# DeltaNet and a multiplicative FFN: the last unit's last two products in two PSUM tiles instead of the two halves of one

## The chip, the cores and the metric

The kernel runs on one core of a Trainium2 chip. The metric is device time in microseconds (us), measured around one execution of the program; the profile is one profiled execution of the same program. Engines are named as the profile names them: PE is the matmul engine (PEld its weight loads), DVE the vector engine, ACT the scalar engine, POOL GpSimd, SP the engine whose queue issues most DMAs.

## What is computed

An attention block (the delta rule, a recurrence over 768 tokens for 4 batches of 8 heads of 48 features) gives a matrix x of 3072 tokens by 384 features. A feed-forward block follows. The change is at the end of the second block:

```python
state = state + bt * einsum('bhd,bhe->bhde', kt, vt - v_old)   # for each token; y = q @ state before it
x = attn_out.transpose(0, 2, 1, 3).reshape(3072, 384)
a = x @ w1                    # 384 x 1024
b = x @ w2
h = a * b @ w3                # 1024 x 1024
out = h @ w_out               # 1024 x 384
```

All arrays are 32-bit floats.

## The kernel before, in words

The sequence is cut into 12 chunks of 64 tokens. Two chunks of all four batches make a unit `u` of 512 tokens, and there are six units (0 to 5; `last` is 5, L893). For a chunk the kernel computes scores, an inverse and the state; for a unit it then does the feed-forward part. The weights `w3` and `w_out` are multiplied together once, into `w34` (1024 x 384), so that a unit's output is (a * b) @ w34.

`ab` (L772) computes a * b of a unit in eight slabs of 128 features, each 128 x 512. PE makes both factors (L779), ACT copies the first one to SBUF (L791), and DVE multiplies it with the second (L795).

The product with `w34` is done by a scheme with seven products of halves in place of eight (a Strassen scheme). The tokens are cut into two halves `z`, the 1024 features into two halves `f`, and the 384 outputs into two halves `d` of 192. `slab_sums` (L835) makes sums of slabs in place on POOL (L846), `weight_sums` (L810) has made those of the weights once for all units. `o` (L851) lists the seven products, one per step: B11, T4, B21, T1, T2, T3, B22 by the name of the weight. Each is eight matmuls, two blocks of 128 tokens times four blocks of 128 features, accumulated over the features into one PSUM bank (L875). The profile lists two rows of 128x192 for each of these matmuls, so 16 rows make one product.

The products go into banks with one-letter names. In units 0 to 4 there are A (B11 and then B21 added), D (T4), C (T1 and then B22 added) and B (T2 and then T3 added). In the last unit T3 and B22 aren't added to B and C but have places of their own, E and F (L861, L862). E and F come from `two_banks` (L146), which gives a tile of two banks by turns out of two such tiles (the profile calls them ps_w); all the others come from `bank` (L149), one bank by turns out of four (ps_f). Before the change, one call of `two_banks` at E serves both, E as its first bank and F as its second.

`result` (L898) combines the banks on ACT and DVE. In the last unit its steps are, in this order:

- M1 = A after its first product, copied by ACT (L904), and osb(0,0) = A, complete, by ACT (L906), with its store
- U2 = M1 + B, U3 = U2 + E, M1 = U2 + C (all on DVE, L900)
- osb(1,1) = U3 + C, with its store
- osb(1,0) = U3 - D, with its store
- osb(0,1) = M1 + F, with its store

Each `store` (L882) writes a 128 x 384 tile osb, of which there are two, taken by turns, and sends it out with two DMAs on SP's queue (L888). So osb(0,1) takes the tile that osb(1,1) had.

The order of all the work is written out by hand in `ORDER` (L39): each name is a generator, and each mention runs it to its next `yield`. `in_text_order` (L159) then ties each engine's instructions to the order in which they were issued. At the end of the list the steps of the last unit are

```python
... o5 S5 S5 S5 o5 x5 S5 x5 o5 x5 x5 x5 x5 x5 x5 x5 x5
```

where `o5` is a product, `x5` a step of `result` and `S5` a slab sum. The three mentions of `o5` shown here make T2, T3 and B22: F's product stands ahead of U3 = U2 + E in the text. Waits between engines are set by the framework, from the tiles that an instruction reads and writes.

Of the kernel before, what the change touches and what calls it, by code (L numbers as in the profile page):

```python
# [89 lines left out]
def kernel(  # L90
# [47 lines left out]
    def in_turn(pool, shape, tag, n, name, dt=FP32):  # L138

        i = turns.get(tag, -1)  # L140
        while True:
            i = turns[tag] = (i + 1) % n
            if (tag, i) not in held:
                return pool.tile(shape, dt, tag=f"{tag}{i}", name=name, bufs=1)

    def two_banks():  # L146
        return in_turn(psW, [P, 2, 512], "w", 2, "ps_w")

    def bank(shape):  # L149
        return in_turn(psF, shape, "f", 4, "ps_f")  # L150
# [179 lines left out]
    def by_tensor(m, i, src):  # L330
        KQ = KQs[m] if m in KQs else new_KQ(m)
        ps = [bank([P, NR, NP, C]) for z in range(2)]
        for r in range(NR):
            for h in range(H):
                for z in range(2):
                    x = half(z if i else (z + h) % 2)
                    pe.matmul(
                        ps[z][feat(h % 2), r, h // 2, :], lhsT=src[x, r, h, :],
                        rhs=ident[x, x], start=True, stop=True,
                    )  # L340
        yield
        for z in range(2):
            for e in range(2):
                o = KQ[feat(e), NR * z : NR * z + NR, :, i, :].rearrange("p b a t -> p (b a) t")
                x = ps[z][feat(e)].rearrange("p r a t -> p (r a) t")
                if i or e:
                    act.copy(out=o, in_=x)  # L347
                else:
                    dve.tensor_copy(out=o, in_=x)
                yield  # L350
# [69 lines left out]
    def inverse(j):  # L420
# [15 lines left out]
        for s in range(BS - 1):  # L436
            n = BS - 1 - s
            t = in_turn(work, [P, 256], "tb", 2, "tb")
            tv = t[:, 0 : (s + 1) * n].rearrange("p (r t) -> p r t", t=n)
            dve.tensor_tensor(  # L440
                out=tv, in0=V[:, 0 : s + 1, s : s + 1].to_broadcast([P, s + 1, n]),
                in1=U[:, s, s + 1 : BS].unsqueeze(1).to_broadcast([P, s + 1, n]), op=ALU.mult,
            )
            o = V[:, 0 : s + 1, s + 1 : BS]
            dve.tensor_tensor(out=o, in0=o, in1=tv, op=ALU.subtract)  # L445
            yield
# [353 lines left out]
    HB, HF, HD = B // 2, KF // 2, DM // 2  # L800
# [48 lines left out]
    banks = {}  # L849

    def o(u):  # L851
        for z, f, w, n, first in (
            (0, 0, "B11", "A", True),
            (1, 1, "T4", "D", True),
            (0, 1, "B21", "A", False),
            (1, 0, "T1", "C", True),
            (0, 0, "T2", "B", True),
            (1, 1, "T3", "B", False),
            (0, 1, "B22", "C", False),
        ):  # L860
            if u == last and n + w in ("BT3", "CB22"):  # L861
                first, n = True, {"T3": "E", "B22": "F"}[w]  # L862
            if first and n in "EF":
                if n == "E":
                    extra = two_banks()
                banks[u, n] = extra[:, "EF".index(n), 0 : HB * HD].rearrange(
                    "p (b d) -> p b d", b=HB
                )
            elif first:
                banks[u, n] = bank([P, HB, HD])[:]  # L870
            ps = banks[u, n]
            for b in range(HB):
                t0 = (HB * z + b) * P
                for i in range(HF):
                    pe.matmul(  # L875
                        ps[:, b, :], lhsT=abs_[u, HF * f + i][:, t0 : t0 + P], rhs=ws_[w][:, i],
                        start=first and b == i == 0,
                        stop=i == HF - 1 and b == HB - 1, skip_group_check=not first,
                    )
            yield  # L880
# [156 lines left out]
```

## Time and profile before

| what | value |
|---|---|
| device time, three runs | 595.52, 597.24, 598.57 us (median 597.24) |
| the profiled execution | 599.28 us |
| its span, first to last instruction | 597.5 us |
| granted PE clock, mean | 0.976 |
| one product of `o` in the last unit, 16 rows | 2.76 us |
| one sum at L900, 128x384 | 0.55 us |
| end of PE's last matmul | 590.0 us from the span's start |
| last DMA issue on SP | begins at 594.72 us, takes 0.43 us |

The span is what the profile covers; the device time of the same execution has 1.78 us more around it. In the views below, a row gives an engine, a line of the kernel, what was written from what by the names of the tiles (with the number of a tile left out), the shape and a count. "Idle before" is how long the engine stood still ahead of a row, with the releaser that ended it. A chain of waits is followed back from the last instruction, at each step to what released it. Matmul ends are modelled.

### The profile page before, as it was taken

Reading aid. Unit: us, or ns where it says so; the run is one execution under the profiler, and the core shown is the slowest. Engines: PE = TensorE matmul, PEld = TensorE weight load, DVE = VectorE, ACT = ScalarE, POOL = GpSimd, SP = SyncE. Lnnn points to the kernel's source line nnn. Section 1 sums busy time; section 2 is a strip of 40 time slices with the busy share of each in tenths; the row PEclk is TensorE's granted clock in tenths of the full one; section 3 lists DMA queues with packets and bytes.
Section 4 is the critical chain, followed back from the end, with each engine's and each line's share of the span. In section 5 each row is a group of like instructions: output and inputs, shape, how many; then the busy total and the mean of one; then the engine's idle time right before and its main releaser. Section 6 shows DMA issues by size and latency. Waiting matters only on the chain.

```text
span 597.5 us, 19061 instructions
## 1 busy us (share of the span) xinstructions
PE 543.5 (91%) x8188; PEld 378.7 (63%) x8188; DVE 362.0 (61%) x827; ACT 158.8 (27%) x333; POOL 176.3 (30%) x223
## 2 busy tenths in 40 slices
PE   2468998768999999999999989999999999999994
PEld 2355555647888864559844669545697456964484
DVE  3797897659987478753895645865738915110112
ACT  3575353444512301121111212112220112301000
POOL 7553543114355502117011043111170002500060
PEclk9998999879999999999999989999999999999998
DMA  9988986767757454663544335624532030010001
GB/s 245 190 172 257 189 181 134 128 133 160 157 79 101 100 85 106 88 99 46 138 67 89 49 55 105 122 61 59 80 74 69 33 56 4 19 51 0 1 13 40
DMA packets 219507, 57.31 MB, mean 96 GB/s; under 512 B 206656, under 2 KB 212800, under 8 KB 219424
## 3 DMA queue, kind: packets, MB, share of 16 engines
q1 hardware_dynamic: 215232, 55.31, 46.4%
q10 hardware_dynamic: 4192, 0.79, 1.0%
q8 instruction: 64, 1.05, 0.8%
q14 instruction: 19, 0.16, 0.1%
HBM read 43.88 MB, written 11.01 MB: 92 GB/s over the span
## 4 chain that ended last, share of the span: by engine, by line
PE 74%; DMA 9%; DVE 6%; SPq 4%; ACT 3%; issue 3%; POOL 1%; DVEq 0%; ACTq 0%; POOLq 0%
PE ps_f L779 38%; PE ps_f L875 18%; PE ps_w L551 5%; PE ps_w L652 4%; PE ps_w L498 3%; PE ps_f L759 2%; DMA raw<-in_moe_w_dram 2%; DMA raw<-in_moe_w_out_dram 2%; DMA xT<-xT 2%; PE ps_w L367 2%; PE ps_w L373 1%; SPq L202 1%; DVE ps_w L445 1%; DVE tb L440 1%; DMA Vd<-Vb 1%
## 5 line engine op out<-in xcount | busy, mean ns | idle before, releaser
L779 PE MATMUL ps_f<-xT,w2s 128*128 128x512 f32 (+1 forms) x336 | 133.2, 543 | 0.8 <-POOL w2s L715 0.8
L779 PE MATMUL ps_f<-xT,w1s 128*128 128x512 f32 (+1 forms) x336 | 128.1, 533 | 1.6 <-DMA xT<-xT 1.6
L846 POOL TENSOR_TENSOR ab<-ab 128x256 f32<-128x256 f32 x96 | 67.2, 729 | 190.2 <-DVE ab L795 167.4
L779 PEld LDWEIGHTS ps_f<-xT,w1s 128*128 128x128 f32 x336 | 63.2, 190 | 56.7 <-issue 53.2
L779 PEld LDWEIGHTS ps_f<-xT,w2s 128*128 128x128 f32 x336 | 62.7, 191 | 55.4 <-issue 51.1
L791 ACT COPY ab<-ps_f 128x512 f32<-128x512 f32 (+1 forms) x56 | 28.2, 527 | 169.5 <-PE ps_f L779 163.3
L875 PE MATMUL ps_f<-w,ab 128*128 128x192 f32 x368 | 65.2, 331 | 0.1
L875 PEld LDWEIGHTS ps_f<-w,ab 128*128 128x128 f32 x368 | 59.7, 190 | 4.1 <-issue 3.2
L795 DVE TENSOR_TENSOR ab<-ab,ps_f 128x512 f32<-128x512 f32 (+1 forms) x56 | 32.7, 603 | 47.2 <-PE ps_f L779 47.1
L440 DVE TENSOR_TENSOR tb<-Vb,Ub 128x31 f32<-128x31 f32 (+15 forms) x124 | 45.4, 366 | 18.2 <-DMA Ub<-Ud 14.9
L759 PE MATMUL ps_f<-w2s,w3T 128*128 128x384 f32 x128 | 45.1, 504 | 4.5 <-POOL w2s L715 2.4
L875 PE MATMUL ps_f<-room,ab 128*128 128x192 f32 x272 | 48.0, 330 | 0.8 <-DVE room L900 0.8
L445 DVE TENSOR_TENSOR Vb<-Vb,tb 128x31 f32<-128x31 f32 (+15 forms) x124 | 45.0, 363 | 4.3
L875 PEld LDWEIGHTS ps_f<-room,ab 128*128 128x128 f32 x272 | 44.1, 190 | 1.6 <-issue 1.1
L673 ACT COPY xT<-ps_w 48x256 f32<-48x256 f32 x96 | 30.5, 366 | 52.9 <-PE ps_w L652 52.4
L759 PEld LDWEIGHTS ps_f<-w2s,w3T 128*128 128x128 f32 x128 | 24.3, 197 | 21.1 <-POOL w2s L715 3.4
L270 POOL TENSOR_TENSOR sq<-ktok 128x384 f32<-128x384 f32 x24 | 20.4, 852 | 56.0 <-DVE Vb L445 26.9
L367 PE MATMUL ps_w<-KQ 48*64 48x128 f32 x384 | 29.9, 292 | 1.1 <-ACT KQ L347 1.1
L715 POOL TENSOR_TENSOR w<-w,raw 128x512 uint32<-128x512 uint32 x16 | 20.8, 1305 | 34.1 <-DVE w L711 21.2
L373 PE MATMUL ps_w<-KQ 48*64 48x64 f32 x768 | 30.3, 232 | 0.1
L537 POOL TENSOR_TENSOR vtok<-vtok,n 128x384 f32<-128x384 f32 x24 | 20.2, 852 | 33.6 <-DMA vtok<-in_v_dram 33.6
L373 PEld LDWEIGHTS ps_w<-KQ 48*64 48x64 f32 x768 | 27.3, 145 | 0.4 <-ACT KQ L347 0.3
(110 smaller groups left out, 658.7 us busy)
## 6 DMA issues: line engine op xcount, KB each, us to landing
raw<-in_moe_w_dram SPq DMA_DIRECT2D x16, 512.0 KB, 6.6
vtok<-in_v_dram SPq DMA_DIRECT2D x24, 192.0 KB, 4.3
raw<-in_moe_w_dram SPq DMA_DIRECT2D x24, 192.0 KB, 4.4
out_dram<-osb SPq DMA_DIRECT2D x48, 96.0 KB, 2.4
ktok<-in_k_dram SPq DMA_DIRECT2D x44, 96.0 KB, 3.8
raw<-in_moe_w_out_dram SPq DMA_DIRECT2D x8, 384.0 KB, 3.8
Ud<-U SPq DMA_DIRECT2D x48, 64.0 KB, 2.7
Ub<-Ud SPq DMA_DIRECT2D x6, 512.0 KB, 4.0
```

Of the source, the lines that this page charges most:

```text
L367: pe.matmul(ps[half(z), 0, n : n + 128], lhsT=x[:, 0, :], rhs=x.rearrange("p j t -> p (j t)"), start=True, stop=True,)
L373: pe.matmul(ps[half(z ^ j), 1, n + C * j : n + C * j + C], lhsT=x[:, 0, :], rhs=x[:, j, :], start=True, stop=True,)
L440: dve.tensor_tensor(out=tv, in0=V[:, 0 : s + 1, s : s + 1].to_broadcast([P, s + 1, n]), in1=U[:, s, s + 1 : BS].unsqueeze(1).to_broadcast( ...
L445: dve.tensor_tensor(out=o, in0=o, in1=tv, op=ALU.subtract)
L551: pe.matmul(out(ps, r, h, z), lhsT=lhs(r, h, z), rhs=rhs(r, h, z), start=True, stop=True,)
L673: act.copy(out=xT[f, p:NP:2, b : b + NR, cc, :].rearrange("p a r t -> p r a t"), in_=pyv[f, z, b : b + NR],)
L759: pe.matmul(ps[:, 0:DM], lhsT=w3Ts[jc, kc // 4][:, kc % 4 * P : kc % 4 * P + P], rhs=wo[:, kc], start=(kc == 0), stop=(kc == KF - 1),)
L779: pe.matmul(ps[:].rearrange("p b c t -> p b (c t)"), lhsT=w[:, m, js], rhs=x[:, m, :, c0:c1].rearrange("p b c t -> p b (c t)"), start=(m = ...
L791: act.copy(out=t, in_=ps)
L795: dve.tensor_tensor(out=t, in0=t, in1=ps, op=ALU.mult)
L846: pool.tensor_tensor(out=o_, in0=x_, in1=y_, op=op)
L875: pe.matmul(ps[:, b, :], lhsT=abs_[u, HF * f + i][:, t0 : t0 + P], rhs=ws_[w][:, i], start=first and b == i == 0, stop=i == HF - 1 and b = ...
```

## The change

E and F each get a `two_banks` tile of their own, and each uses the first bank of it. Since these tiles come by turns out of two, E gets one of them and F the other. The list of steps is the same.

```diff
@@ -861,9 +861,7 @@
             if u == last and n + w in ("BT3", "CB22"):
                 first, n = True, {"T3": "E", "B22": "F"}[w]
             if first and n in "EF":
-                if n == "E":
-                    extra = two_banks()
-                banks[u, n] = extra[:, "EF".index(n), 0 : HB * HD].rearrange(
+                banks[u, n] = two_banks()[:, 0, 0 : HB * HD].rearrange(
                     "p (b d) -> p b d", b=HB
                 )
             elif first:
```

Lines behind the change move up by two.

## The prediction

> **What bounds the kernel now.** I read the page's busy shares first, then the chain of waits over the last 38 us, then the waits and the timeline of the last 23 us, then the busy time in single stretches of it.
>
> ```profile
> PE 543.5 (91%) x8188; PEld 378.7 (63%) x8188; DVE 362.0 (61%) x827; ACT 158.8 (27%) x333; POOL 176.3 (30%) x223
> PE 74%; DMA 9%; DVE 6%; SPq 4%; ACT 3%; issue 3%; POOL 1%; DVEq 0%; ACTq 0%; POOLq 0%
> ```
>
> PE sets the pace nearly everywhere: 91% busy and 74% of the chain. A change that leaves PE's work alone can only gain where PE isn't the end of the chain. The chain's last pieces show such a place:
>
> ```profile
> 584.79 5.21 PE ps_w L875 x32
> 590.00 0.02 issue
> 590.02 0.07 DVE room L900
> ...
> 590.96 0.56 DVE osb L900
> ...
> 591.91 1.73 DMA out_dram<-osb
> ...
> 593.76 0.55 DVE osb L900
> ```
>
> (Columns: start, length, what.) PE's last product ends at about 590.0 and the span at 597.5. In these 7.5 us PE has nothing to do: DVE makes the last sums, a store lands, DVE makes the very last sum, and it is stored too. This tail is what the change touches. The timeline shows when its parts start:
>
> ```profile
> 584.62 2.76 PE L875 MATMUL ps_w<-room,ab 128*128 128x192 f32 x16
> 584.88 0.56 DVE L900 TENSOR_TENSOR room<-room,ps_f 128x384 f32<-128x384 f32 x1 [12.37 <-PE ps_f L875]
> ...
> 587.22 2.76 PE L875 MATMUL ps_w<-w,ab 128*128 128x192 f32 x16
> 590.02 0.55 DVE L900 TENSOR_TENSOR room<-room,ps_w 128x384 f32<-128x384 f32 x1 [4.59 <-PE ps_w L875]
> 590.50 0.55 DVE L900 TENSOR_TENSOR room<-room,ps_f 128x384 f32<-128x384 f32 x1
> 590.96 1.01 DVE L900 TENSOR_TENSOR osb<-room,ps_f 128x384 f32<-128x384 f32 x2
> 593.76 0.55 DVE L900 TENSOR_TENSOR osb<-room,ps_w 128x384 f32<-128x384 f32 x1 [1.79 <-DMA out_dram<-osb]
> ```
>
> The first PE row is product E (weight T3), the second F (weight B22); both carry the name ps_w because they are halves of one tile. DVE's sum U3 = U2 + E stands in the fifth row. E is complete at 584.62 + 2.76 = 587.38 and U2 at 584.88 + 0.56 = 585.44, yet the sum starts at 590.02, just after F's end at 587.22 + 2.76 = 589.98. It reads nothing of F. So it waits 2.6 us for a product that it doesn't need; the waits put 4.6 us of DVE's idle time down to ps_w.
>
> ```profile
> DVE room L900 <- PE ps_w L875: 4.6, 1, 4.6
> DVE osb L900 <- DMA out_dram<-osb: 1.8, 1, 1.8
> ```
>
> The second line is the other wait that matters: the last sum (M1 + F) writes an osb buffer of which there are two, and it has to wait until the store of (1,1), which leaves from that buffer, has landed.
>
> **What the Trainium skill says.** "PSUM — Partial Sum Buffer", in "Summary: rules for kernel authors", says that PSUM may be read while a matmul runs if the read is from another bank, and that semaphores should guard it by bank. E and F are in two banks already in the kernel before, so the bank isn't what holds the sum; the shared tile is. The trace agrees that reading beside a running product is usual: the sum at 584.88 reads bank B while E is being written. "Perfetto Trace Analysis", in "Tensor Engine Instruction (MATMUL, LD_WEIGHTS)", says that a matmul's profiled end is an estimate and that its semaphore goes up after it. The trace agrees in size: readers start 0.04 to 0.10 after the modelled end of a product. "DMA: Bandwidth & Descriptors", in "Anatomy of one DMA", puts a fixed cost of about 2 us on a DMA, most of it the receipt of the write. Here the stores show 1.6 to 1.7 us from issue to landing (below), and the trace's number is used.
>
> **The change part by part.**
>
> *Work.* The instruction lists of the two built programs have the same matmuls, sums and DMAs in the same order on every engine. What differs is the waits of the last few. Before, PE posts once for E and F together, by 16 matmuls, and the sum U2 + E waits for that count (4132). After, PE posts by 8 after E and by 8 after F; U2 + E waits for 4124, E's end, and the last sum, M1 + F, waits itself for 4132. Cost of posting: PE's queue gets no new instruction, so nothing. The second tile's place was last used by an earlier chunk's products, read long before; PE's list of waits gains none. Nothing before E is touched, so up to 584.62 I count no change.
>
> *The sum U2 + E.* It is now released by E at 587.38. The lag from the end of a product to its reader is 0.10 for the sum at 584.88 (B ends at 582.02 + 2.76 = 584.78), 0.04 for the read at 579.62 (A ends at 576.82 + 2.76 = 579.58) and 0.04 at 590.02. So it starts at 587.42 to 587.48, I take 587.45. U2 (585.44) is no limit. Gain at this step: 590.02 - 587.45 = 2.57, between 2.54 and 2.60.
>
> *The sums behind it.* U2 + C, U3 + C and U3 - D are queued behind it on DVE and wait for nothing but it: C and D are complete, and the buffer of (1,0) is the one that the store issued at 580.13 has left long ago. They start at the same distances: 0.48 and 0.94 after it, so the first osb sum starts at 588.39 in place of 590.96. All this now lies beside F's matmuls.
>
> *The store of (1,1).* SP issues it when that sum ends; in the trace at 591.53, two DMAs, then the two of (1,0) behind them. Issue, transfer and receipt take until about 593.67, after which the last sum starts at 593.76: 2.80 from the first osb sum to the last. Nothing else is in SP's queue. It moves as a block to 588.96, and the last sum would be let go at 588.39 + 2.80 = 591.19.
>
> *The last sum's new wait.* M1 + F now waits for F as well: 589.98 plus 0.04 to 0.10, about 590.05. That is 1.14 before 591.19, so the landing still decides and the new wait costs nothing. Its cover is the (1,1) store: if that were gone, F would be next, and the most that this change could give is 593.76 - 590.02 = 3.74. The wait comes with one more semaphore instruction in DVE's queue ahead of the sum. The queue's such steps show as 0.05 in the chain (593.67), but the added one waits for the first DMA of the pair, which should land before the second, so I take 0; at the worst 0.05. Behind the waiting sum on DVE there is nothing; its reader is SP with the last two DMAs, so this wait would count in full if it were late.
>
> *After the last sum.* From 593.76 to 597.5 are 3.74 us: the sum, two issues, landing, the closing waits. They move as they are. One wait of the closing list falls away (the one for PE), worth one 17 ns semaphore instruction at most; I take 0.
>
> Sum: 2.57 (2.49 to 2.62). The profiled execution took 599.28 with a span of 597.5, so 1.78 lie around the span; it would take 599.28 - 2.57 = 596.71 with a span of 594.9. The profiled execution is 2.04 above the median of the runs shown, and the tail is the same work in each, so I subtract the same amount there: 597.24 - 2.57 = **594.67**, 0.43% less.
>
> **The rivals.**
>
> *F is held up by the sums beside it (part of the gain).* Four sums now read PSUM while F is written, 0.48 + 0.46 + 0.46 + 0.55 = 1.95 us of them. If PE stood still for all that, F would end at 591.93, the last sum would start at 591.97, and the gain would be 593.76 - 591.97 = 1.79: 595.45. Against it: product E has a sum beside it and F has none, and both keep the same pace.
>
> ```profile
> 584.80:587.40 2.60, 2.60 (x18) 2.60 (x18) 0.56 (x1) 0.00 (x0) 0.00 (x0) 1.00 0.00 0
> 587.40:590.00 2.60, 2.59 (x16) 2.29 (x15) 0.00 (x0) 0.00 (x0) 0.00 (x0) 1.00 0.00 0
> ```
>
> (Stretch, length, busy time of PE, weight loads, DVE, ACT, POOL, granted clock.)
>
> *The change doesn't do what it says (597.24).* If U2 + E were held by something besides the shared tile, for instance if E's count became visible only once PE's stream ran dry, it would still start at 590.02. For it: the waits name ps_w, which can't tell E from F. Against it: B's reader started 0.10 after B's end with E already streaming.
>
> *Slower: the store under running matmuls lands late.* The (1,1) store used to run with PE idle; now it runs beside F's matmuls and weight loads, and the last sum waits for it. If it landed as late as the slowest kind of DMA on the page (the moe weights, a median of 6.6) and not in 1.7, the last sum would go 4.9 later, to 596.1, which is 2.3 after 593.76: 599.6. It decides from the point where the landing takes 1.7 + 2.57 = 4.3. Against it: the first two of the eight last stores were issued at 580.13 with PE at full pace, and no landing stands out.
>
> ```profile
> DMA to landing us min/median/max: 1.6/1.7/1.7
> ```
>
> The 6.6 is of 16 transfers among heavy traffic; in the last slices of the page the queues are nearly empty.
>
> **How the numbers follow.** Forecast 0.88, held-up F 0.06, no effect 0.03, late store 0.03. A measurement of this kernel can tell about 0.5% from no change, which is 2.99 us, and the forecast of 2.57 lies just within that. The three runs of before reach from 1.72 below the median to 1.33 above it, so that a difference of two such medians may be off by about 1.2: 0.42 more than forecast comes about 4 times in 10, so 0.88 is parted into 0.36 faster and 0.52 same. Held-up F (0.06, gain 0.3%) and no effect (0.03) go to same nearly whole, the late store (0.4% slower, more if it is worse) half to slower. Faster 0.37, same 0.60, slower 0.03.
>
> The predicted time is 594.7. The range goes from 593.2 to 596.6: 1.5 below the forecast for the spread of the runs, and above it over the held-up F (595.45) with 1.15 of spread on top; it leaves out most of no effect and the late store, and the far ends of the spread.
>
> **What would show it right or wrong.** Right: the sum that follows U2 starts 0.04 to 0.10 after E's modelled end, not F's; three more sums run beside F's matmuls; F's matmuls still take 2.60 from first start to the end of the stretch; the first store of (1,1) is issued before F has ended; the last sum still waits for that store's DMA (about 1.8 us of DVE idle) and not for PE; from PE's last matmul to the end of the span 4.9 us in place of 7.5. Wrong: U2 + E starting at F's end (no effect); F longer than 2.76 or the last sum released by PE (held up); a landing well over 1.7 (late store); or a difference in start times ahead of product E, which nothing in the change explains.

## The result and the profile after

The changed kernel takes 594.9 us (median of 20 runs) and the kernel before 597.38 us (20 runs beside them). The ratio is 0.9952 with a 95% interval of 0.9930 to 0.9974: about 2.9 us less (1.6 to 4.2), against a forecast of 2.57. The ratio leaves out the runs in a slower state, more than 1.5% above the fastest of the same kernel (three of the changed kernel's 20), and so it isn't just the quotient of the two medians. The interval lies wholly below 1, so this is a gain, though a small one beside the spread of the changed kernel's runs (589.96 to 601.20 us). The profiled execution took 597.89 us with a span of 596.2.

The timeline of the changed kernel's end, row by row what was shown of before:

```profile
585.85 2.76 PE L873 MATMUL ps_w<-room,ab 128*128 128x192 f32 x16
586.11 0.55 DVE L898 TENSOR_TENSOR room<-room,ps_f 128x384 f32<-128x384 f32 x1 [12.37 <-PE ps_f L873]
...
588.45 2.76 PE L873 MATMUL ps_w<-w,ab 128*128 128x192 f32 x16
588.66 0.55 DVE L898 TENSOR_TENSOR room<-room,ps_w 128x384 f32<-128x384 f32 x1 [1.99 <-PE ps_w L873]
589.13 0.55 DVE L898 TENSOR_TENSOR room<-room,ps_f 128x384 f32<-128x384 f32 x1
589.59 1.01 DVE L898 TENSOR_TENSOR osb<-room,ps_f 128x384 f32<-128x384 f32 x2
592.39 0.55 DVE L898 TENSOR_TENSOR osb<-room,ps_w 128x384 f32<-128x384 f32 x1 [1.79 <-DMA out_dram<-osb]
```

Read it against the first row, E's product. U3 = U2 + E (fourth row) starts at 588.66, only 0.05 after E's end (585.85 + 2.76 = 588.61), while F (third row) runs until 591.21. Its idle time has shrunk from 4.59 to 1.99. The next three sums follow beside F. The last sum is still released by the landing of a store, after the same 1.79 of idle time.

The absolute times mislead here: E starts at 585.85 in this execution and at 584.62 in the one of before, so that the spans differ by 1.4 only. To compare the ends, all times below count from the start of E's first matmul. (Before: U3 at 590.02 - 584.62 = 5.40, end of the span at 597.54 - 584.62 = 12.92. The pages give spans to 0.1 only; 597.54 and the other ends below are the spans that the traces hold, to 0.01. The expectations quoted below use 12.88, from the rounded 597.5.)

| from E's start, us | before | after |
|---|---|---|
| U3 = U2 + E starts | 5.40 | 2.81 |
| F's matmuls start, end | 2.60, 5.36 | 2.60, 5.36 |
| first osb sum starts | 6.34 | 3.74 |
| last sum M1 + F starts | 9.14 | 6.54 |
| last store's first DMA is issued | 9.72 | 7.12 |
| end of the span | 12.92 | 10.32 |

The last store's first DMA is issued at these rows of SP's queue, before and after:

```profile
594.34 0.33 SPq L888 DMA_DIRECT2D out_dram<-osb  x1
592.97 0.33 SPq L886 DMA_DIRECT2D out_dram<-osb  x1
```

U3 and all that follows it have moved by 2.59 to 2.60, the end of the span included. F's matmuls stand where they stood. The chain of waits of the changed kernel shows what the end now hangs on:

```profile
586.02 2.61 PE ps_w L873 x16
588.63 0.02 issue
588.66 0.07 DVE room L898
...
589.59 0.56 DVE osb L898
590.15 0.02 issue
590.16 0.33 SPq L886
...
590.54 1.73 DMA out_dram<-osb
...
592.39 0.55 DVE osb L898
```

Before, this chain had 32 rows of ps_w, E and F; now it has 16, E alone. PE's very last product has left the path.

### The profile page after: what moved, and what is told of

Its sections match the earlier page's. It is cut to its first block, busy times and chain, and to the rows that moved or that the text cites. A ratio compares the mean times of both kernels' runs of the same rounds, so it can differ in the third digit from the quotient of the medians.

```text
span 596.2 us, 19061 instructions
## 1 busy us (share of the span) xinstructions
PE 545.3 (91%) x8188; PEld 381.0 (64%) x8188; DVE 363.5 (61%) x827; ACT 158.8 (27%) x333; POOL 176.3 (30%) x223
## 4 chain that ended last, share of the span: by engine, by line
PE 78%; DMA 10%; SPq 5%; DVE 3%; issue 2%; ACT 1%; POOL 1%; ACTq 0%; DVEq 0%; POOLq 0%
PE ps_f L779 41%; PE ps_f L873 19%; PE ps_w L551 5%; DMA raw<-in_moe_w_dram 4%; PE ps_w L652 4%; PE ps_f L759 3%; PE ps_w L498 3%; SPq L230 2%; PE ps_w L367 2%; PE ps_w L373 2%; DMA ktok<-in_k_dram 1%; DMA Ub<-Ud 1%; DMA Ud<-U 1%; SPq L699 1%; DMA X<-in_q_dram 1%
## 5 line engine op out<-in xcount | busy, mean ns | idle before, releaser
L779 PE MATMUL ps_f<-xT,w1s 128*128 128x512 f32 (+1 forms) x336 | 129.6, 538 | 2.6 <-DMA xT<-xT 2.6
L779 PE MATMUL ps_f<-xT,w2s 128*128 128x512 f32 (+1 forms) x336 | 131.4, 537 | 0.0
L873 PE MATMUL ps_f<-room,ab 128*128 128x192 f32 x272 | 49.6, 337 | 0.8 <-DVE room L898 0.8
L759 PE MATMUL ps_f<-w2s,w3T 128*128 128x384 f32 x128 | 46.3, 515 | 3.4 <-POOL w2s L715 3.3
L445 DVE TENSOR_TENSOR Vb<-Vb,tb 128x31 f32<-128x31 f32 (+15 forms) x124 | 46.4, 374 | 4.3
L873 PEld LDWEIGHTS ps_f<-room,ab 128*128 128x128 f32 x272 | 45.8, 195 | 1.6 <-issue 1.1
```

Source lines behind the costliest of these rows:

```text
L759: pe.matmul(ps[:, 0:DM], lhsT=w3Ts[jc, kc // 4][:, kc % 4 * P : kc % 4 * P + P], rhs=wo[:, kc], start=(kc == 0), stop=(kc == KF - 1),)
L779: pe.matmul(ps[:].rearrange("p b c t -> p b (c t)"), lhsT=w[:, m, js], rhs=x[:, m, :, c0:c1].rearrange("p b c t -> p b (c t)"), start=(m = ...
L873: pe.matmul(ps[:, b, :], lhsT=abs_[u, HF * f + i][:, t0 : t0 + P], rhs=ws_[w][:, i], start=first and b == i == 0, stop=i == HF - 1 and b = ...
```

## The experiments

The theory: DVE waited for the tile, not for the bank or the product; with that wait gone, the landing of the (1,1) store is next, and F's end is 1.14 behind it. The rivals were that PE's stream sets the end whatever the tiles, that the sums slow F, and that something else held U3. The table gives the four profiles of the first set from E's start; the kernel before has 5.40, 5.36, 9.14 and 12.92.

| kernel | U3 starts | F ends | last sum | end | gain at the end | ratio of times to before |
|---|---|---|---|---|---|---|
| one tile, sum first | 2.80 | 6.34 | 6.54 | 10.33 | 2.59 | 0.9924 (0.9890 to 0.9958) |
| two tiles, F twice | 2.80 | 7.96 | 8.00 | 11.78 | 1.14 | 0.9956 (0.9934 to 0.9977) |
| two tiles, third osb | 2.80 | 5.36 | 5.40 | 9.43 | 3.49 | 0.9938 (0.9917 to 0.9958) |
| one tile, third osb | 5.40 | 5.36 | 7.27 | 12.02 | 0.90 | 0.9983 (0.9957 to 1.0009) |

The intervals of the ratios are 2.4 to 4.1 us wide, since the executions differ by more than that ahead of E. Three of the four hold the gain that the end of the profile shows. The one of F twice doesn't: a gain of 1.14 would be a ratio of 0.9981, and the interval ends at 0.9977, 0.2 us away. One such miss among several 95% intervals may be chance. But in all seven comparisons of this document the times fell by more than the ends of the profiles did, by 0.1 to 1.9 us, and whether something ahead of E also gains isn't shown. So the times say that there is a gain, and what each edit does to the tail is read from the profiles, of which there is one for each kernel.

### One tile, and the sum ahead of F in the list of steps

```diff
-S5 S5 o5 x5 S5 x5 o5 x5 x5 x5 x5 x5 x5 x5 x5
+S5 S5 o5 x5 S5 x5 x5 o5 x5 x5 x5 x5 x5 x5 x5
```

> One tile for E and F as in the kernel before, but the step U3 = U2 + E stands ahead of F's product in the list of steps. Times count from the start of E's first matmul; in the kernel before U3 starts at 5.40, the last sum at 9.14 and F's matmuls at 2.60, in the changed one at 2.81, 6.54 and 2.60. Theory (the tile is the unit of waiting, and the order of the text says who waits for whom): U3 starts at 2.81, and now F waits until U3 has been read, so that PE stands still: F starts at 3.4 to 3.7 and ends at 6.2 to 6.5. That lies just within the 1.14 of slack ahead of the landing, so the last sum starts at 6.54 to 6.6 and the gain over the kernel before is 2.5 to 2.6 us, as with two tiles. Rival A (the gain needs PE to run through, because PE sets the end): the standing still is lost in full, the last sum starts at 7.4 or later, gain 1.7 or less. Rival B (U3 is held by something besides the tile): U3 starts at 5.4, no gain or a loss.

The timeline of this kernel:

```profile
579.41 2.76 PE L875 MATMUL ps_w<-room,ab 128*128 128x192 f32 x16
...
582.21 0.55 DVE L900 TENSOR_TENSOR room<-room,ps_w 128x384 f32<-128x384 f32 x1 [1.99 <-PE ps_w L875]
...
582.91 2.84 PE L875 MATMUL ps_w<-w,ab 128*128 128x192 f32 x16 [0.74 <-DVE room L900]
...
585.95 0.56 DVE L900 TENSOR_TENSOR osb<-room,ps_w 128x384 f32<-128x384 f32 x1 [1.79 <-DMA out_dram<-osb]
```

U3 starts at 2.80 with the single tile too, and with E and F in the banks that they had before, so rival B falls, and so does the thought that F's new place made the gain. (PE stands idle when U3 starts here, so this run alone couldn't exclude that E's count shows only once PE's stream runs dry. The changed kernel does: there U3 starts with F already running.) In exchange PE now stands still for 0.74, released by DVE: F mustn't write its half until U3 has read the other half, though the two are in different banks. That shows the tile as the unit of waiting, in both directions, with the order of the text deciding who waits. (The counterpart, the sum first with two tiles, was not run.) F ends at 6.34, 0.98 later than before, and yet the last sum starts at 6.54 as in the changed kernel. So rival A falls as well: 0.98 more on PE cost nothing, since the slack was 1.14.

### Two tiles, F computed twice

```diff
-            for b in range(HB):
+            for b in [*range(HB)] * (2 if n == "F" else 1):
```

> The changed kernel with F's product computed twice, so that F ends 2.60 later; the output is the same. It measures the slack that was put at 1.14 and the point from which the last sum's new wait for F decides. Times from the start of E's first matmul. Theory: U3 stays at 2.81, F ends at 7.96, and the last sum is let go by PE at 8.00 to 8.06 instead of 6.54 by the landing: 1.46 to 1.52 later than in the changed kernel, which leaves 1.1 of the gain over the kernel before. Rival (the landing decides with much more room than 1.14, or the sums slow F): last sum at 6.54, no loss; or later than 8.1.

```profile
583.60 2.76 PE L873 MATMUL ps_w<-room,ab 128*128 128x192 f32 x16
...
586.20 5.36 PE L873 MATMUL ps_w<-w,ab 128*128 128x192 f32 x32
586.40 0.56 DVE L898 TENSOR_TENSOR room<-room,ps_w 128x384 f32<-128x384 f32 x1 [1.99 <-PE ps_w L873]
...
591.60 0.55 DVE L898 TENSOR_TENSOR osb<-room,ps_w 128x384 f32<-128x384 f32 x1 [3.25 <-PE ps_w L873]
```

The last sum has changed its releaser: PE in place of the DMA, at 591.60, 8.00 from E's start (583.60). F has become 2.60 longer and the last sum 1.46 later, which leaves 2.60 - 1.46 = 1.14 of slack, the forecast's figure. Beyond it the new wait counts in full.

### Two tiles and a third buffer for the last store

```diff
-        osb = in_turn(ffn, [P, DM], "o", 2, "osb")
-        make(osb[:])
+        if (u, z, d) == (last, 0, 1):
+            osb = ws_["spare"]
+        else:
+            osb = in_turn(ffn, [P, DM], "o", 2, "osb")[:]
+        make(osb)
```

`spare` is an unused part of the room that holds U3.

> The changed kernel with a third buffer for the last store, so that the last sum doesn't wait for the landing of (1,1). Times from the start of E's first matmul. Theory: the next thing that is late is F's end at 5.36: the last sum starts at 5.40 to 5.46 and ends at 5.95 to 6.01. SP's queue issues four DMAs for (1,1) and (1,0) from 4.32 to 6.10, so the last store is issued at about 6.1 to 6.2 instead of 9.72 in the kernel before and 7.1 in the changed one: gain 3.5 to 3.6 over the kernel before, about 1.0 over the changed one. Rival (the landing wasn't the limit, the DVE queue was): no gain over the changed kernel.

```profile
581.13 2.76 PE L873 MATMUL ps_w<-room,ab 128*128 128x192 f32 x16
...
583.73 2.76 PE L873 MATMUL ps_w<-w,ab 128*128 128x192 f32 x16
583.93 0.55 DVE L901 TENSOR_TENSOR room<-room,ps_w 128x384 f32<-128x384 f32 x1 [1.99 <-PE ps_w L873]
...
586.53 0.55 DVE L901 TENSOR_TENSOR room<-room,ps_w 128x384 f32<-128x384 f32 x1 [0.65 <-PE ps_w L873]
587.31 0.86 SPq L889 DMA_DIRECT2D out_dram<-room  x2
```

The last sum (the row at 586.53) waits for PE alone and starts at 5.40. That is also the answer to the rival of sums that slow F: in the kernel before, the sum behind F started at 5.40 with no sum beside F, and here it does so with four beside it, 1.95 us of them. The stretches of this kernel say the same, the first with E's product, the second with F's (columns as in the prediction, PE's busy time first):

```profile
581.13:583.73 2.60, 2.60 (x18) 2.60 (x17) 0.56 (x1) 0.00 (x0) 0.00 (x0) 1.00 0.00 0
583.73:586.33 2.60, 2.60 (x18) 2.47 (x16) 1.95 (x4) 0.00 (x0) 0.00 (x0) 1.00 0.01 4
```

The last store is issued at 6.18, 0.23 after its sum has ended (5.95), because SP is then still busy with the four DMAs before it. The gain is 3.54 by that issue, and 3.49 at the end.

### One tile and a third buffer

The same edit on the kernel before.

> The kernel before with the third buffer for the last store and nothing else. Times from the start of E's first matmul. Theory: U3 still waits for F's end and starts at 5.40; the last sum follows straight behind the other sums at 7.26 instead of 9.14 and ends at 7.8. But SP is issuing the four DMAs of (1,1) and (1,0) from 6.91 to 8.7, so the last store is issued at 8.7 to 8.8 instead of 9.72: gain 0.9 to 1.0, not the 1.9 of the sum. Together with the run of two tiles and a third buffer it shows whether the two waits are in series: 2.6 for the tile and 1.0 for the buffer make 3.6 if they are. Rival (only the buffer's wait matters, the tile's is hidden behind it): gain 2.6 or more.

```profile
582.25 2.76 PE L875 MATMUL ps_w<-room,ab 128*128 128x192 f32 x16
...
584.85 2.76 PE L875 MATMUL ps_w<-w,ab 128*128 128x192 f32 x16
587.65 0.55 DVE L903 TENSOR_TENSOR room<-room,ps_w 128x384 f32<-128x384 f32 x1 [4.59 <-PE ps_w L875]
...
589.16 1.77 SPq L891 DMA_DIRECT2D out_dram<-osb  x4
589.52 0.55 DVE L903 TENSOR_TENSOR room<-room,ps_w 128x384 f32<-128x384 f32 x1
591.03 0.86 SPq L891 DMA_DIRECT2D out_dram<-room  x2
```

U3 is back at F's end. The last sum comes 1.87 earlier than before, but it ends at 590.07 and its store is issued at 591.03 only: SP's four issues take 1.77. So 0.94 remains by the issue, 0.90 at the end. By the issues, 2.60 for the tile and 0.94 for the buffer make 3.54, exactly what the two together gave: the two waits are in series.

### The last store on ACT's queue

```diff
-        yield from store(u, 0, 1, plus("M1", "F") if u == last else plus("U2", "C"))
+        if u == last:
+            yield from store(u, 0, 1, plus("M1", "F"), act.dma_start)
+        else:
+            yield from store(u, 0, 1, plus("U2", "C"))
```

> The kernel with two tiles and the third buffer, and the last store's two DMAs issued from ACT's queue instead of SP's. Times from the start of E's first matmul. In the run with the third buffer the last sum started at 5.40 and ended at 5.95, and SP, busy with four other issues, took the last store up at 6.18. Theory (SP's queue is what is late by then): ACT issues it at 5.97 to 6.0, a gain of about 0.2 over that run, 3.6 over the kernel before by the end of the span (12.88 there). Rival (the end of the last sum decides, SP's queue was ready): no difference.

```profile
587.57 2.76 PE L873 MATMUL ps_w<-room,ab 128*128 128x192 f32 x16
...
592.97 0.55 DVE L901 TENSOR_TENSOR room<-room,ps_w 128x384 f32<-128x384 f32 x1 [0.65 <-PE ps_w L873]
593.56 0.86 ACTq L889 DMA_DIRECT2D out_dram<-room  x2
```

From E's start at 587.57 the store is issued at 5.99 in place of 6.18, and the span ends at 9.24 in place of 9.43: the forecast 0.2, and SP's queue was what was late. The ratio to before is 0.9931 (0.9906 to 0.9956). The span of this execution, 596.8, is long because E starts late in it; from there to F's end the granted clock is 1.00, as it is in the run with the third buffer alone.

### F in two banks by token blocks, and the last sum in halves

```diff
+            elif first and n == "F":
+                banks[u, n] = (two_banks()[:, 0, 0:HD], bank([P, HB, HD])[:, 0])
...
-        yield from store(u, 0, 1, plus("M1", "F") if u == last else plus("U2", "C"))
+        if u < last:
+            yield from store(u, 0, 1, plus("U2", "C"))
+        else:
+            for b in range(HB):
+                o_ = ws_[f"O{b}"]
+                dve.tensor_tensor(
+                    out=o_, in0=ws_["M1"][:, HD * b : HD * b + HD], in1=banks[u, "F"][b], op=ALU.add
+                )
+                t0 = b * S + u * 2 * C
+                act.dma_start(out=out[t0 : t0 + P, d_half(1)], in_=o_)
+            yield
```

> As the run on ACT's queue, but F's two token blocks go into two banks (the second one into a bank of the other pool that has been read), and the last sum is made in two halves of 192 columns, each with its buffer and its DMA on ACT's queue. Times from the start of E's first matmul. Theory: the first half is there at 3.9 and its sum follows the others on DVE at 4.75; the second half's sum starts at F's end, 5.40, takes about 0.35 instead of 0.55 and leaves one DMA to issue instead of two: the last DMA starts at about 5.77 instead of 6.5, 0.7 earlier than with the third buffer alone; end of the span at 8.7 to 8.8, that is 4.1 under the kernel before. Rival (the landing of several stores at once is the limit): no gain over the run on ACT's queue.

```profile
579.43 2.76 PE L877 MATMUL ps_w<-room,ab 128*128 128x192 f32 x16
...
583.33 1.46 PE L877 MATMUL ps_f<-w,ab 128*128 128x192 f32 x8
583.75 1.79 SPq L891 DMA_DIRECT2D out_dram<-osb  x4
584.10 0.35 DVE L927 TENSOR_TENSOR room<-room,ps_w 128x192 f32<-128x192 f32 x1
584.48 1.08 ACTq L931 DMA_DIRECT2D out_dram<-room  x2
584.84 0.35 DVE L927 TENSOR_TENSOR room<-room,ps_f 128x192 f32<-128x192 f32 x1 [0.39 <-PE ps_f L877]
```

The first half's sum starts at 584.10 while F's second half runs, and the second half's sum takes 0.35. The last DMA is issued at 585.22, which is 5.79 from E's start (579.43), and the span ends at 8.78: 4.14 under the kernel before, 1.54 under the changed one and 0.46 under the run on ACT's queue, so the rival falls. By times it is 592.94 us against 597.73 of the kernel before (ratio 0.9926, 0.9899 to 0.9953); with the changed kernel only the ends compare it. PE's end is what its last sum waits for.

## Why the prediction was right

*The sum U2 + E.* Taken at 2.83 from E's start (between 2.80 and 2.86); measured 2.81, and 2.80 or 2.81 in the five runs that keep the sum free of F. The gain there was 2.59, within the 2.54 to 2.60 given. (The counts 4124 and 4132 of the forecast stand in no trace here; what the traces show is when the sum is let go.)

*The sums behind it, and the store.* They moved as a block: the first osb sum by 2.60, the last sum by 2.60. No landing got longer with PE at work, which was the slower rival. Of the eight DMAs of the last stores in the changed kernel:

```profile
DMA to landing us min/median/max: 1.6/1.7/1.7
```

*The last sum's new wait* cost nothing, with 1.14 of cover. The changed kernel only shows that the cover exists; the run with F twice shows its size, and the run with the sum first shows 0.98 of it used at no cost. If the store's buffer is taken out of the way, F is what is late next, as stated.

*The bound of 3.74.* It was given as the most that freeing the landing could bring. The start of the last sum did move by 3.74 (9.14 to 5.40), but 3.54 of that reached the store's issue and 3.49 the end of the span. The step "nothing else is in SP's queue" holds for the changed kernel and not for that bound: four issues of 1.8 us in all were in front.

*The closing part*, taken to move unchanged, is 596.17 - 592.39 = 3.78, and in the kernel before 597.54 - 593.76 = 3.78 too: it did. (The forecast's 3.74 comes from the rounded 597.5.)

*The size in the times.* The forecast of 2.57 lies inside the interval of 1.6 to 4.2, and so does 2.99. Whether the gain is just under 0.5% or at it can't be told from these runs; the profiles say 2.6, 0.44%. That the predicted 594.7 lies 0.2 from the measured median of 594.9 is luck, since the gain in the times is known to 1.3 us either way.

*A sign of being wrong that did show.* The prediction named a difference in start times ahead of E as one, and E starts 1.23 later in the changed kernel's profile; that is why its span came out at 596.2 and not at the forecast 594.9. The other profiles speak against an effect of the change: with one tile for E and F, E starts at 579.41, 582.25 and 584.62, with two between 579.43 and 587.57.

## What to carry to other kernels

If a reader starts at the end of a product that it doesn't use, look for a tile that both share: the wait was for the tile, though the halves lay in different banks, and a tile each or another order of the text removed it. Before counting such a gain, write down for each later step what it waits for next and by how much; here 1.14 us lay between the landing of a store and the end of PE, and that margin said how much more work on PE cost nothing (0.98 with the sum first) and what came through beyond it (1.46 of the 2.60 with F twice). When the body of a kernel varies by more than the effect, count times from an instruction that stands just ahead of what the change touches.

## What was not expected

The executions differ much more ahead of the change than the change is worth. E's product starts between 579.41 and 587.57 us in the eight profiled executions, although no edit touches an instruction ahead of it. Part of the difference is there early. The copies of M1 (one per unit) in the run with the last store on ACT's queue and in the run with F in halves start, the first and the last of them, at:

```profile
L905 ACT COPY room<-ps_f x6: 479/480/480, 199.1 to 577.4; 128x384 f32<-128x384 f32 x6
L907 ACT COPY room<-ps_f x6: 478/479/479, 194.4 to 569.3; 128x384 f32<-128x384 f32 x6
```

4.7 us of the 8.1 are there in the first unit. Over the first 200 us the granted clock is 0.94 in the first of these two and 0.96 in the second, so the clock may have a part in it; what makes the difference wasn't tried and stays open. From E on, what two kernels should have in common repeats to some hundredths of a us: U3 free of F starts at 2.80 or 2.81 in all six profiles that have it.
